# Batch 4's first layer as seven products instead of eight, and a rewritten order of all later work, in an attention and two-layer kernel

## The chip, the cores and the metric

The kernel runs on one core of a Trainium2 chip. Its engines each take their own instructions in order: TensorE (PE in the profile, with its weight loads as PEld), VectorE (DVE), ScalarE (ACT), GpSimd (POOL) and SyncE (SP). They wait for each other through semaphores. SP and POOL issue most of the DMA transfers. The metric is the device time of one execution in microseconds.

## The reference

Inputs are q, k and v of 8 batches, 12 heads, 448 positions and 64 features, and two weight matrices of 768 x 2048 and 2048 x 768, all float32.

```python
scores = scale * np.matmul(q, k.transpose(0, 1, 3, 2))      # scale = 1 / sqrt(64)
attn = np.maximum(scores, 0.0) ** 2 / S                      # no softmax
x = np.matmul(attn, v)             # then heads side by side: 3584 rows of 768
h = x @ w_in
g = 0.5 * h * (1.0 + erf(h * inv_sqrt2))
out = g @ w_out                    # 3584 rows of 768, float32
```

## The kernel before

**Attention.** The loads on POOL's queue turn q, k and v into bfloat16 on their way in. Heads are handled in three groups of four (g = 0 to 2) and keys in seven pieces (i = 0 to 6). One step of `add_steps` is four matmuls into a PSUM tile `ps` (tag "w", three buffers), a relu on ACT or DVE, and a square on DVE. The square goes into one of 14 buffers of `apool`. When the seven steps of a group are there, `add_av` makes 28 matmuls into `pav`, and two copies put the result into `xT`, which is x transposed.

**Turning q and k.** Scores need q and k with features on the partitions. Batches 0 and 1 are turned by TensorE. For batches 2 to 7 `add_T_dma` (line 657) does it with DMA transposes on SP's queue, one for k and one for q of each head group ("turn"), and then a half-swap of q: the upper 64 partitions are copied below and the lower above, either by two DMAs on SP or by two copies on DVE (`swapped`, line 681). A score step needs the turned k and the swapped q of its group. Natural-layout buffers of q and k are single from batch 2 on, so a load of batch b + 1 into them waits for batch b's turns. `add_gate` (line 706) puts a small copy on POOL that waits for a turn, so that loads behind it on POOL wait too.

**First layer, plain.** `add_f1` makes one of 16 tiles of a batch: six matmuls of 448 columns into `psh`, and a GELU on ACT into `h_sb`, a ring that holds two batches.

**First layer, block form.** `add_blocks` and `add_block` split x, w_in and h into 2 x 2 blocks and make them with seven block products instead of eight, at the price of sums. The sums of w_in are made once (`add_wsums`). Those of x are four per batch (`xsum`, tile `xs`). The seven products of one part (six matmuls of 224 columns each, line 999, PSUM tiles `pb` with tag "w") share three bank pairs a, b and c. Between products DVE or ACT takes a bank's content away (`passed`, tile `part`), and ACT makes four GELUs. A batch has four such parts: m4 = 0 and 4, and y = 0 and 1 for the two banks of a tile. A part that needs a buffer of `h_sb` waits until the readers of the batch two before it are done.

**Second layer.** Rows 0 to 255 are made plainly (`add_plain`, line 1268). Then `add_group` makes 256 rows at a time (groups 1 to 13), again with seven products, of eight matmuls of 384 columns (line 1173). Their sums of h are `s_sb`, those of w_out `t_sb`. The results go through `osb` (three buffers) to the output by stores on SP.

**Which batch is made how.** Batches 0 to 4 are plain in the first layer. Batches 5, 6 and 7 are in block form at the end. While attention runs, PE alternates between attention steps and pieces of the two layers. After the last attention there are only block products and groups.

**What sets the order.** Each piece of work is an `Op` with the engines that may do it. The program lists them, and the text `ORDER` says which stands next: a letter for the engine (P, A, D, G for POOL, S for SP) and the number of the `Op` in the order in which the program made them. Every engine works through its own words in that order. The batch-2 turns and swaps have the numbers 228 to 236: for each head group the turn of k, the turn of q, and the swap. So S229 is the turn of q of group 0, D230 its swap on DVE.

Of the kernel before, what the change touches and what calls it, by code (L numbers as in the profile page):

```python
# [9 lines left out]
BF16 = mybir.dt.bfloat16  # L10
# [6 lines left out]
HS = S // 2  # L17
# [69 lines left out]
G0 G1 G3 G4 G1428 G7 G121 A10 P11 D13 G2 A16 P17 D12 P14 G117 D18 P42 P39 G6 P21 D15 P19 A43 G118  # L87
P36 D22 P33 A40 P23 G5 D20 P25 D41 P54 A37 G122 D24 Z1056 D26 A34 P66 P57 D38 A55 D44 G8 P63 P29
P27 A58 D67 P69 P51 D35 A64 P48 D30 P31 D65 A70 P45 D28 D32 A52 P78 D59 G9 P133 D46 A49 P108 D68
D47 P111 A79 P75 D134 P129 A109 D50 P81 P131 D56 A76 P102 D112 P84 G125 A82 D71 P72 D53 A103 G120  # L90
P60 D130 A85 D104 P93 A73 P135 A61 D110 A74 A62 P96 D132 P105 G124 P141 D83 D77 A97 P168 A94 D106
P165 P90 A142 G119 P143 D86 D113 A169 G126 D107 P114 A166 D80 P87 D98 A91 D95 P171 A144 D115 P137
A88 D92 A116 P99 D89 P156 A172 D136 P159 A100 D138 P145 G128 A157 A101 D160 P162 P186 D167 P174
A146 P251 D163 A175 P243 D158 A187 D176 G148 A252 D170 P183 P195 P189 G147 D173 A244 P259 G151
A196 D184 G154 P253 D161 A260 G150 D164 P139 A190 P198 A254 P180 P177 D140 A181 D199 P219 P216
# [4 lines left out]
G153 G238 P350 A357 G149 P348 G270 A292 A351 P285 P300 P303 G272 A349 P354 G241 A301 P364 A304  # L100
A355 P312 P318 P362 A365 P370 D319 D281 A363 D296 P358 A313 D236 D290 A286 P282 P306 A371 P315
P352 A359 D307 P360 A353 P376 A361 P368 A316 A377 D317 P372 D314 A369 D308 P366 D293 A373 P378
A283 A367 D284 P374 S234 A379 D390 P382 D278 S399 A375 D391 D392 P380 D417 D418 D305 G242 G152
D302 D287 G269 S398 P327 P339 D320 P297 G271 D396 G155 A328 D383 P333 G274 P384 D381 G273 D298
A340 A299 D393 A334 D394 P330 P324 P309 D329 P387 D419 A331 D335 A385 S402 A310 D395 D311 S386
A325 P342 P336 S401 P321 D397 D400 D388 A343 D332 P421 A322 D337 A323 P423 D420 D338 D422 S405
P446 P443 D341 P449 P425 D424 D344 A450 S404 S403 S406 P427 G413 D444 G275 A426 G409 S389 D447
P429 D326 D428 P452 P455 P345 A456 D453 P440 P437 D445 P431 D430 A441 D560 P433 D346 A347 D432
S435 P473 A438 P461 P470 D434 S436 P509 G407 G408 G410 A471 D474 P513 D448 G412 A462 S542 D457
A510 G411 P479 D454 P476 P464 G415 A514 P519 D472 D442 G414 A465 D439 P517 A520 D477 P515 A480  # L110
D451 A518 S541 P485 P467 P458 A468 P491 A516 S545 P511 D459 A486 D561 P523 A492 D487 A512 D460
P503 P494 P500 D563 A524 P525 D463 S544 A495 D466 P521 D469 A526 D481 P531 D504 A522 D478 P527
A532 D501 P537 D475 S548 A528 D505 P529 D502 A538 D493 S547 S543 S546 S549 P488 P497 P482 A498
D489 P606 G556 P600 G552 G416 P535 A483 A530 G550 P533 D601 G551 A607 D484 A536 G553 D490 G555
P539 D496 G554 D499 P609 G559 P603 P506 G558 A604 D610 G557 P624 A534 P639 D562 P564 A540 D605
A507 P566 A640 D625 D565 D508 P615 P612 P618 D567 P568 A616 D613 P570 D617 A569 D611 D614 P572
S705 D619 P657 D571 P627 P636 S704 P574 D580 D573 A637 D620 P576 D608 A658 D575 S578 A628 P584
D581 S708 D638 D577 P586 D583 S579 D582 P630 D602 P633 P621 D626 A634 D631 P651 A585 S707 P642
P588 D632 D587 A643 D659 P590 D629 A652 A622 D641 D591 P648 A623 D644 P666 P663 A589 S711 D653
P592 D635 A664 S710 S706 S709 S712 G719 P594 G715 A649 D667 D593 P654 P660 P645 A655 D661 P769  # L120
P763 D595 P596 S598 D725 A770 G713 G714 A646 P672 D764 G716 D597 S599 P674 G718 D665 D650 A673
G717 G721 A647 D656 P772 P778 P775 G720 D662 A675 P678 S868 A776 D779 P676 D668 A773 D771 P766
D777 P787 P669 S867 A767 D788 A679 P781 P790 A677 D774 P682 A670 D723 D768 P684 A782 A671 D724
A683 D765 P680 D783 A791 D780 P796 P799 P784 A681 S871 A800 D797 P793 P802 P688 D803 D804 S870
D798 D789 D792 S874 S873 S869 S872 S875 G882 G722 A785 A685 P686 A794 A689 A786 P811 P823 P805
A687 P690 D795 A806 P692 A691 D824 P698 D726 A812 D807 A693 P696 D801 A699 P814 P817 P808 A697
A815 D818 P820 P906 G878 P694 A809 G876 G877 P702 D907 G879 A695 A810 G881 P700 G880 A821 G884
A703 P826 P829 D822 P912 A701 P727 A827 P729 D828 A728 D813 P731 A913 D730 A830 D816 P733 D819
D825 P921 D831 P909 P832 A910 D922 P918 P936 D732 G885 P735 D734 A833 G883 D911 A919 D834 P924
P915 A937 P737 D736 A916 D925 P930 P933 D938 P942 P739 D743 A931 D738 S741 D744 P747 A934 D745  # L130
D740 S742 P749 D917 A748 D935 S979 P751 D914 A943 D920 D750 S978 P753 D944 A752 D746 S982 P755
D923 D926 D754 P757 D932 D908 P939 P948 P927 D758 S981 A940 D949 P960 P945 D941 P835 A928 D756
D950 A946 P759 A929 S761 D961 S985 D947 P957 P954 P951 A836 D760 S984 S980 S983 S986 A958 D955
P963 P966 P839 D956 A952 S762 D953 A967 P837 D959 A840 P969 D964 P972 P987 A838 D888 P841 A973
P843 D988 D965 A842 D989 P845 A970 D962 A844 D974 P847 D971 A846 D1067 P1002 D968 P990 P975 A1003
D991 A848 P993 P996 P851 D976 A994 A977 P999 D997 P1014 P1005 A852 D1004 P849 D995 D992 P853 D886
A850 D1068 P857 D998 A1000 A854 P855 D1015 A1006 D1001 P1017 D1007 P1026 P1008 D1070 A1027 D1018
P1029 A856 P1011 P859 A858 D1059 A1009 D1028 P863 D1019 A1030 A860 D1031 P865 A1012 D1060 A864
A1010 P1035 D887 P1047 P1020 D1016 A866 P861 A1048 P890 D1021 A1036 A862 D1063 D1022 P1023 P1041
P1044 A891 D1013 P892 A1024 D1042 P1053 A1045 D1025 P1050 P1032 D1069 A1051 D1054 P1038 P1071  # L140
A1033 D1062 P894 D1049 A1072 D1043 P1088 D893 A1039 P1073 A1034 D1066 A895 P1079 A1089 D1040
P1090 D889 P1096 P1075 D1091 P896 D1055 D1074 D1181 P1094 D1052 P1077 D897 P1092 P898 D1095 D1078
P1082 D1064 P1099 P900 D1061 D899 D1097 P902 D1083 D1100 P1105 D1080 D901 S904 P1102 A1076 D1179
P1085 A1106 D1139 P1122 A1093 D1046 A1084 P1107 D1037 P1124 A1123 D903 S905 P1109 A1081 D1086
P1126 D1103 A1087 P1113 D1108 P1130 D1125 A1110 P1128 A1127 D1065 P1111 A1104 D1140 A1098 P1056
D1180 D1129 D1112 P1133 D1131 P1143 D1057 D1114 P1119 D1058 P1136 D1134 D1291 P1116 D1144 P1183
D1120 P1200 D1137 P1185 D1117 P1202 A1184 D1141 A1201 P1191 D1182 P1187 D1203 P1145 D1186 P1189
P1206 P1208 P1147 D1190 D1207 D1146 P1194 D1192 P1211 D1209 P1149 D1195 P1214 D1212 D1148 P1217
D1150 P1197 D1142 P1151 A1218 A1115 D1198 A1118 P1221 D1215 A1135 P1234 D1152 A1121 P1219 A1132
P1236 A1101 A1138 P1153 A1235 D1237 P1238 D1161 P1155 D1220 D1154 S1157 P1240 D1159 P1223 D1156  # L150
S1158 P1163 D1160 D1241 P1245 P1165 D1164 D1224 P1228 P1167 D1166 D1162 D1246 P1169 D1229 D1168
P1225 P1171 D1170 D1253 P1173 D1172 D1226 P1175 D1251 P1242 P1231 A1239 P1204 A1222 P1303 A1227
D1243 P1248 D1176 S1178 A1188 P1320 A1205 D1252 P1295 A1210 D1174 S1177 A1244 D1232 P1312 A1199
D1292 P1255 A1230 D1249 A1296 D1254 A1313 P1297 D1293 A1193 P1314 A1196 P1299 A1256 P1257 A1233
D1298 A1213 D1315 A1216 P1301 P1316 D1258 P1318 P1261 D1319 P1259 D1302 D1304 D1294 P1309 D1262
P1323 A1260 A1250 P1263 D1310 A1247 D1324 P1306 D1321 P1265 D1264 D1307 P1326 P1329 P1346 D1327
P1331 D1271 P1267 A1347 D1272 A1330 P1350 P1348 D1268 S1270 P1333 P1275 D1349 D1266 S1269 D1273
P1277 D1276 P1279 D1274 D1332 D1278 P1352 P1335 A1280 P1281 P1283 D1282 P1285 D1365 D1353 D1336
# [239 lines left out]
def kernel(  # L398
# [738 lines left out]
    def add_group(g):  # L1137
# [116 lines left out]
        for bb in bs:  # L1254
            readers.setdefault(bb, []).extend(mine)
# [287 lines left out]
```

## Time and profile before

| what | us |
|---|---|
| median of 3 runs (lowest, highest) | 369.7 (369.43, 370.05) |
| the profiled execution | 368.93 |
| its span, first to last instruction | 367.2 |
| PE, DVE, ACT, POOL busy | 358.1, 291.2, 191.8, 63.5 |
| psh, plain first layer, 516 matmuls | 96.3 |
| ps and pav, scores and attention output, 756 matmuls each | 47.9 and 36.3 |
| last attention output on PE ends | 263.7 |

A busy time is the union of an engine's instructions. Matmuls overlap, so a single one's duration (0.34 us) is longer than its share of the stream. A DVE instruction of 617 ns is followed by the next after 535 ns. The chain of waits follows the last instruction back to what released it. The timeline gives start, length, engine, line and operands, and in brackets how long the engine had stood idle and what ended that.

### The profile page before, as it was taken

The numbers are of one execution on the slowest core, as the hardware profiler recorded it, in microseconds if no ns is written. First come the engines' busy times: TensorE is split into PE (matmuls) and PEld (weight loads), VectorE is DVE, ScalarE is ACT, GpSimd is POOL, SyncE is SP. The second block draws the span as 40 slices with busy tenths as digits, with TensorE's granted clock in tenths as the row PEclk, the third lists the DMA queues.
The fourth block names the chain that finished last, engine by engine and source line by source line (L and its number), as shares of the span: only waits on it lengthen the run. The fifth ranks groups of instructions, "written<-read, shape, count | busy, mean of one in ns | idle before, by whom it ended". The sixth has DMA issues, their size and how long they took to land.

```text
span 367.2 us, 8476 instructions
## 1 busy us (share of the span) xinstructions
PE 358.1 (98%) x3560; PEld 222.3 (61%) x3560; DVE 291.2 (79%) x488; ACT 191.8 (52%) x312; POOL 63.5 (17%) x101
## 2 busy tenths in 40 slices
PE   8889999999999999999999999999999999999994
PEld 7666654455544555544455544478888787867662
DVE  3999882689996899998579999999977766667753
ACT  4987867637377544678665466951414134133100
POOL 8565134410600700501310000000000000000000
PEclk9999999999999999999999999999999999999998
DMA  9999999999999999999949770000200211022233
GB/s 172 200 200 204 188 141 203 191 197 157 162 258 172 185 167 188 175 247 161 190 68 201 142 158 2 2 2 5 83 2 1 87 48 40 14 73 87 86 86 88
DMA packets 74406, 46.19 MB, mean 126 GB/s; under 512 B 38400, under 2 KB 70912, under 8 KB 74368
## 3 DMA queue, kind: packets, MB, share of 16 engines
q0 software_dynamic: 32912, 22.47, 42.2%
q1 hardware_dynamic: 40816, 22.67, 29.5%
q8 instruction: 28, 0.46, 0.5%
q10 hardware_dynamic: 640, 0.51, 0.4%
q14 instruction: 10, 0.08, 0.1%
HBM read 45.61 MB, written 11.01 MB: 154 GB/s over the span
## 4 chain that ended last, share of the span: by engine, by line
PE 95%; ACT 3%; issue 1%; DVE 0%; DVEq 0%
PE pso L1173 33%; PE psh L855 26%; PE pb L999 13%; PE ps L742 10%; PE pav L803 9%; ACT a_sq L754 3%; PE pso L1268 3%; PE spin L1340 1%; PE tp L638 0%; PE tp L610 0%; DVE qT L516 0%; DVEq L1538 0%; DVE osb L1207 0%; DVE zero L1324 0%
## 5 line engine op out<-in xcount | busy, mean ns | idle before, releaser
L754 ACT ACTIVATE a_sq<-ps 128x896 bf16<-128x896 f32 (+1 forms) x116 | 102.5, 923 | 44.1 <-PE ps L742 41.1
L763 DVE TENSOR_TENSOR a_sq<-a_sq 128x896 bf16<-128x896 bf16 x169 | 97.1, 614 | 8.0 <-ACT a_sq L754 7.7
L855 PE MATMUL psh<-xT,win_sb 128*128 128x448 bf16 (+1 forms) x516 | 96.3, 340 | 0.0
L855 PEld LDWEIGHTS <-win_sb 128*128 128x128 bf16 x516 | 47.9, 98 | 45.9 <-issue 9.8
L756 DVE TENSOR_SCALAR a_sq<-ps 128x896 bf16<-128x896 f32 (+1 forms) x53 | 57.0, 1078 | 16.6 <-PE ps L742 16.4
L1173 PEld LDWEIGHTS <-s_sb 128*128 128x128 bf16 x424 | 40.7, 98 | 25.7 <-issue 1.8
L865 ACT ACTIVATE h_sb<-psh 128x448 bf16<-128x448 f32 x80 | 43.5, 550 | 22.3 <-PE psh L855 22.0
L742 PE MATMUL ps<-qT,kT 64*64 64x448 bf16 (+1 forms) x756 | 47.9, 336 | 1.0 <-ACT a_sq L754 0.4
L1036 DVE TENSOR_TENSOR part<-pb,part 128x448 f32<-128x448 f32 x60 | 35.2, 617 | 13.6 <-PE pb L999 11.5
L1173 PEld LDWEIGHTS <-h_sb 128*128 128x128 bf16 x312 | 29.8, 98 | 20.9 <-issue 3.2
L1173 PE MATMUL pso<-wout_sb,h_sb 128*128 128x384 bf16 x208 | 38.1, 326 | 0.0
L1173 PE MATMUL pso<-wout_sb,s_sb 128*128 128x384 bf16 (+2 forms) x216 | 38.1, 320 | 0.0
L1173 PE MATMUL pso<-t_sb,s_sb 128*128 128x384 bf16 x208 | 38.1, 326 | 0.0
L803 PE MATMUL pav<-a_sq,v_sb 64*64 64x448 bf16 (+1 forms) x756 | 36.3, 329 | 1.3 <-issue 1.1
L1207 DVE TENSOR_TENSOR osb<-pso,p_sb 128x384 f32<-128x384 f32 x39 | 21.5, 551 | 13.0 <-PE pso L1173 11.2
L742 PEld LDWEIGHTS <-kT 64*64 64x64 bf16 x756 | 18.6, 105 | 21.1 <-issue 16.2
L999 PEld LDWEIGHTS <-win_sb 128*128 128x128 bf16 x288 | 27.5, 98 | 2.9 <-issue 0.7
L803 PEld LDWEIGHTS <-v_sb 64*64 64x64 bf16 x756 | 21.1, 107 | 13.0 <-issue 2.3
L1045 ACT ACTIVATE h_sb<-part 128x448 bf16<-128x448 f32 x36 | 18.4, 576 | 19.0 <-DVE part L1036 18.9
L710 POOL COPY gate<-qT 128x16 bf16<-128x16 bf16 x15 | 5.2, 345 | 100.2 <-DMA qT<-nq 79.9
L518 ACT CAST xT<-pav 128x448 bf16<-128x448 f32 (+1 forms) x38 | 18.3, 500 | 7.7 <-PE pav L803 6.3
L999 PEld LDWEIGHTS <-ws 128*128 128x128 bf16 x216 | 20.8, 98 | 1.2
(58 smaller groups left out, 300.5 us busy)
## 6 DMA issues: line engine op xcount, KB each, us to landing
nk<-in_k_dram POOLq DMA_DIRECT2D x23, 224.0 KB, 10.3
nq<-in_q_dram POOLq DMA_DIRECT2D x21, 224.0 KB, 10.2
v_sb<-in_v_dram POOLq DMA_DIRECT2D x5, 672.0 KB, 9.1
qT<-qT SPq DMA_DIRECT2D x28, 112.0 KB, 2.6
out_dram<-osb SPq DMA_DIRECT2D x8, 336.0 KB, 3.0
v_sb<-in_v_dram POOLq DMA_DIRECT2D x9, 224.0 KB, 9.4
out_dram<-osb SPq DMA_DIRECT2D x7, 288.0 KB, 3.1
out_dram<-osb SPq DMA_DIRECT2D x8, 240.0 KB, 3.0
```

The costliest lines, as they stand in the source:

```text
L742: nc.tensor.matmul(ps[64 * j : 64 * j + 64, e, x * w : x * w + w], kT[r, g, i * 128 + 64 * j : i * 128 + 64 * j + 64], moving, start=True, ...
L754: A.activation(ar, ps, AF.Relu, scale=c_att)
L756: V.tensor_scalar(ar, ps, c_att, 0.0, op0=mybir.AluOpType.mult, op1=mybir.AluOpType.max,)
L763: V.tensor_mul(box["a2"][:, :, :used], ar, ar)
L803: nc.tensor.matmul(pav[0][o2 : o2 + 64, e, :w], vt[b][r, 2 * g + e, bass.ts(i, D)], box["a2"][r, y, o : o + w], start=(i == 0), stop=(i == ...
L855: nc.tensor.matmul(ph[:, x * n : x * n + n], win_sb[:, kd, bass.ts(m + x, 128)], xT[b][:, kd, c], start=(kd == 0), stop=(kd == KD - 1),)
L865: A.activation(h_ring()[:, m : m + nm, o + c.start : o + c.stop], box[0][:, :S].rearrange("p (x n) -> p x n", x=nm), AF.Gelu,)
L999: nc.tensor.matmul(bank[name][:, y, z * HS : z * HS + HS], w[:, k, bass.ts(mm, 128)], right()[:, k], start=first and k == 0 and z == 0, st ...
L1036: V.tensor_add(get(to), ps(name), get(other))
L1045: A.activation(h_ring()[:, m : m + 2, o + half[c].start : o + half[c].stop], src().rearrange("p (x n) -> p x n", x=2), AF.Gelu,)
L1173: nc.tensor.matmul(box[bank][:, n0:n1], left()[:, kf], right()[:, kf, n0:n1], start=bool(need) and kf == 0, stop=kf == K2 - 1, skip_group_ ...
L1207: V.tensor_add(out()[:, n0:n1], box[bank][:, n0:n1], other()[:, n0:n1])
```

## The change

Batch 4 moves from the plain form to the block form and into the end: its 16 tiles are no longer spread over attention. The list at the end of the program is built without weaving groups between block products. The x sums of batches 6 and 7 share one buffer, and those of 4 and 5 take the place of kT. Readers and writers of the h ring are now tracked by half batches of 224 rows. `ORDER` is new throughout. In it some half-swaps move from SP to DVE: of the 18, 14 were on SP before and 6 are now. The gates on POOL stand in other places.

```diff
-P245 A178 G123 G127 A220 D217 P207 A179 P210 P204 D191 A246 P261 S229 A211 D208 P247 D182 A205
-S228 D209 A262 D197 P213 P222 P192 D200 S232 A248 P263 D221 A223 D206 P249 D224 A264 D188 P255
-D212 A250 P257 D193 A214 A256 D194 P265 D218 A258 D185 P201 D230 D215 A266 G237 S231 G239 P225
-A202 A203 P276 P279 P267 D233 D226 S235 A277 A227 P291 D280 P288 P294 A268 P356 G240 A295 D289
...
+D181 A199 D188 P216 D178 D197 P245 P219 A220 D179 A217 D185 P247 S228 A246 P210 P204 P207 A211
+A208 A248 S235 D205 P261 S232 P222 P213 D200 D221 D191 A262 P192 A214 P263 S231 P255 A264 D182
+D223 D206 A193 D218 P257 A256 D194 P249 D215 A258 D212 D209 P201 S234 S229 D224 D230 G270 P225
...
@@ -873,7 +875,8 @@
-        old = readers.get(b - 2, [])
+        hs = (0, 1) if half is None else (half,)
+        old = [o for x in hs for o in readers.get((b - 2, x), [])]
...
@@ -952,13 +957,19 @@
-                    tag = "qT" if b == B - 1 else "kT"
-                    box["t"] = tpool.tile([128, 4, K1, HS], BF16, tag=tag, name="xs")
+                    if b < B - 2:
+                        box["t"] = tpool.tile([128, 4, K1, HS], BF16, tag="kT", name="xs")
+                    else:
+                        if not xsums:
+                            xsums.append(
+                                tpool.tile([128, 2, 4, K1, HS], BF16, tag="qT", name="xs2")
+                            )
+                        box["t"] = xsums[0][:, b - B + 2]
...
-        gone = [o for (bb, *_), o in QK.items() if bb == (B - 2 if b == B - 3 else B - 1)]
+        gone = [o for (bb, *_), o in QK.items() if bb == (B - 2 if b == B - 4 else B - 1)]
...
@@ -1433,7 +1450,7 @@
-    F1B = {2: 1, 3: 2, 4: 3, 5: 4}
+    F1B = {2: 1, 3: 2, 4: 3}
...
-    add_wsums(at(B - 1, 1), [F1[B - 4, m, None] for m in range(KF)])
+    add_wsums(at(B - 1, 1), [F1[B - 5, m, None] for m in range(KF)])
...
-    end = woven(add_blocks(B - 3), add_group(7))
-    end += add_group(8)
-    end += woven(add_blocks(B - 2), add_group(9))
-    g10 = add_group(10)
-    end += g10 + woven(add_blocks(B - 1), add_group(11))
-    end += add_group(12) + add_group(13)
+    end = add_blocks(B - 4) + add_group(7)
+    end += add_blocks(B - 3) + add_group(8) + add_group(9)
+    end += add_blocks(B - 2) + add_group(10)
+    end += add_blocks(B - 1) + add_group(11) + add_group(12) + add_group(13)
```

In the old words batch 2's turns stand as S229, S228, S232, S231, S235, and S234 later. In the new ones they stand as S228, S235, S232, S231, S234 and S229, with D230 right behind.

More of the change, by code (lines that the diff above doesn't have):

```diff
@@ L104 @@
[L104 to L145, printed above, removed]
@@ new lines @@
+P297 A328 P333 D392 P339 A334 P382 D298 A375 D329 A340 D317 A299 P330 P324 P309 A325 P380 D417
+D320 A331 D310 A383 D311 D418 D335 P342 D341 P336 P321 D332 S402 D393 P384 A322 D400 S401 A381
+A337 D326 D396 G407 D394 P387 G237 A385 A343 G409 G240 D420 S386 G275 A323 D344 S405 G408 D419
+P443 D338 D388 P446 S404 A444 P421 D395 A447 G412 S389 P449 D397 P345 G411 A450 G242 D445 D403
+A422 P452 P437 A346 S542 P423 D347 A453 A438 P455 D424 P440 P425 D456 A441 D442 P473 P470 A426
+P461 D454 P427 D462 A474 A471 P429 D439 D457 D428 P464 P479 D430 P476 A480 D448 P431 D451 A465
@@ new lines @@
+D1020 P1041 A1040 D1030 D1008 P1058 A1057 D1011 P868 D1059 P1024 D1042 P1045 A1025 A1026 P1060
+D1129 D1031 D1032 D867 P1062 P1043 P1047 D1063 A1044 D1029 P870 A1061 D1046 P1064 D1034 P1050
+P1067 D1048 D1065 P1073 D1051 P1090 D1068 P1053 D1033 P1075 A1074 A1091 A1049 P1092 D1054 P1094
+D1093 P1077 D1076 A1078 A1066 P1070 D871 P1079 D1071 P1096 D869 A1072 A1095 A1055 P1081 D1097
+A1052 S872 S873 P1098 D1080 A1069 P1131 D1082 P1084 D1128 A1083 P1101 D1099 P1148 A1100 P1104
+D1085 D1102 A1149 P1087 A1103 D1331 A1132 P1133 D1105 D1088 A1086 P1150 P1135 D1134 A1106 P1139
@@ L166 @@
+P1417 D1416 A1379 D1423 P1419 D1418 D1424 P1383 D1420 P1400 S1422 P1427 S1421 P1429 D1428 D1384
+D1425 P1431 D1430 A1385 A1368 P1433 D1432 A1362 D1401 D1426 P1435 A1402 D1434 D1445 P1437 D1436
+D1443 P1439 D1438 D1444 S1441 P1447 D1440 S1442 P1449 D1448 P1451 D1450 D1446 P1453 D1452 S1463
+P1455 D1454 P1457 D1456 P1459 D1458 P1460 D1461 D1462 S1465 S1464 S1466
 """
@@ L939, in add_wsums @@
             WS[m0] = {1: s1, 2: s2, 3: s3, 4: s4}
+    xsums = []
     def add_blocks(b):
@@ L973, in add_blocks @@
         TS = {1: t1, 2: t2, 3: t3, 4: t4}
-        old = readers.get(b - 2, [])
         atoms = []
@@ L979, in add_blocks @@
                 ms = range(m4 + 2 * y, m4 + 2 * y + 2)
-                todo.append(add_block(b, m4, y, ms, bank, x, t, TS, xs, old, half))
+                todo.append(add_block(b, m4, y, ms, bank, x, t, TS, xs, half))
             for p in zip(*todo):
@@ L986, in add_blocks, with add_block @@
         return atoms
-    def add_block(b, m4, y, ms, bank, x, t, TS, xs, old, half):
+    def add_block(b, m4, y, ms, bank, x, t, TS, xs, half):
         tmp = {}
@@ L1051, in gelu @@
             d = 0.19 + 0.00069 * S
+            old = readers.get((b - 2, c), [])
             o = sch.add((("ACT", d, d + 0.14),), fn, deps + old, frees=frees, bias=GELU_BIAS)
@@ L1144, in h @@
             return h_ring()[:, i * K2 : i * K2 + K2, o : o + 128]
-        done = [o for (bb, *_), o in GL.items() if bb in bs]
+        hs = {t // HS for r in rows for t in (r[0], r[-1])}
+        done = [
+            o for (bb, m, h), o in GL.items()
+            if bb in bs and (isinstance(m, int) and h is None
+                             or 2 * bb + (h if isinstance(m, int) else m[1]) in hs)
+        ]
         sums = SUMS[0] + SUMS[1]
@@ L1253, in add_group @@
                 sch.add((("SP", 0.6, 2.8),), store(0, c, [nc.scalar, nc.sync]), [o])
-        for bb in bs:
-            readers.setdefault(bb, []).extend(mine)
+        for t in sorted({t // HS for r in rows for t in (r[0], r[-1])}):
+            readers.setdefault(divmod(t, 2), []).extend(mine)
         return [(1.3, o) for o in (p1, p6, p2, p7, p5, p4)] + [(1.3 / len(p3), o) for o in p3]
@@ L1289, in add_plain @@
         plain.append(op)
-        readers.setdefault(bb, []).append(op)
+        for t in sorted({128 * t // HS, (128 * t + 127) // HS}):
+            readers.setdefault(divmod(t, 2), []).append(op)
         return op
```

102 lines of the change are left out of this document (62 added, 40 removed).

## The prediction

> **What bounds the kernel now.** I read the page first, then the chain of waits, then the queues where batch 2 begins.
>
> ```profile
> span 367.2 us, 8476 instructions
> PE 358.1 (98%) x3560; PEld 222.3 (61%) x3560; DVE 291.2 (79%) x488; ACT 191.8 (52%) x312; POOL 63.5 (17%) x101
> PE 95%; ACT 3%; issue 1%; DVE 0%; DVEq 0%
> ```
>
> TensorE is busy for 98% of the span and makes 95% of the chain that ends last. From about 20 us to its last product at 362 us it is fed without a break, so work that leaves PE shortens the time, and any new wait of PE lengthens it one for one. The prices are in the chain of waits (start, us, engine and line, count):
>
> ```profile
> 0.99 4.98 PE spin L1340 x45
> ...
> 45.64 5.78 PE psh L855 x30
> 51.42 2.77 PE pav L803 x56
> 54.19 0.38 PE ps L742 x8
> ...
> 104.46 0.69 PE ps L742 x12
> 105.15 2.38 PE psh L855 x12
> ...
> 214.41 0.95 PE ps L742 x12
> ...
> 298.11 4.60 PE pb L999 x48
> ```
>
> A plain first-layer tile (six matmuls on line 855) takes 1.135 us: two take 2.38 and five 5.78, each with 0.11 ahead. A block product (six matmuls of 224 columns, line 999) takes 4.60 / 8 = 0.575. A score step (four matmuls, line 742) takes 0.19, and three take 0.69: going from attention to the other layers, or back, costs 0.11 to 0.12. The 0.95 at 214.41 is the one wait of the body: 0.26 more than three steps.
>
> Batch 2 is the first whose q and k are turned by the DMA queue of SP. This is what SP, POOL and DVE do before PE reaches it (timeline):
>
> ```profile
> 37.30 1.42 POOL L569 DMA_DIRECT2D v_sb<-in_v_dram  x2 [1.53 <-DMA win_sb<-in_moe_w_in_dram]
> 39.88 1.33 SPq L665 DMA_TRANSPOSE qT<-nq  x1
> 41.27 2.86 SPq L665 DMA_TRANSPOSE kT<-nk  x1
> 44.17 4.05 SPq L665 DMA_TRANSPOSE qT<-nq  x1
> 48.27 1.30 SPq L665 DMA_TRANSPOSE kT<-nk  x1
> 49.61 1.30 SPq L665 DMA_TRANSPOSE qT<-nq  x1
> 50.91 0.79 DVE L516 COPY qT<-qT 64x896 bf16<-64x896 bf16 x2
> 51.76 0.65 POOL L710 COPY gate<-qT 128x16 bf16<-128x16 bf16 x1 [13.03 <-DVE qT L516]
> 54.02 0.55 PE L742 MATMUL ps<-qT,kT 64*64 64x448 bf16 x8
> ```
>
> The reader is to see the order: q of head group 0 is turned first (issued 39.88), DVE swaps its halves at 50.91, and PE takes its first scores of batch 2 at 54.02, three microseconds after the swap could begin. The loads set the pace: the two v loads issued at 37.30 and 38.03 landed 9.4 and 10.1 us later, the last at 48.2, and the first turn, issued at 39.88, landed only after 8.8 us, at 48.7. The fifth, issued at 49.61 with nothing before it, landed after 3.0, at 52.6.
>
> **The change, part by part.** *Batch 4 in block form.* 16 tiles of 1.135 leave PE, 18.16 us. In come 4 blocks of 7 products, 28 x 0.575 = 16.10. PE: -2.06.
>
> *Order on PE.* Counted in the built programs, the sequence changes between attention and the other layers 95 times before and 103 times after. 8 x 0.115 = +0.92.
>
> *Other engines.* The built program gives DVE 20 more passes over block banks (617 ns each), 4 more x sums (498), 16 more half-swaps of qT (405, until now DMAs), and 9 fewer relus (1086). DVE rows overlap by 0.08 (four products of 617 ns take 2.22 us in the timeline). With that, batches 3 to 6 hold 98 us of DVE work against 108 of PE (before: 99 against 120); a block's seven products take PE 4.0 us and DVE 2.7. I put these at nothing: PE's own work hides them. If that cover were gone, only what exceeds PE would count. Bounds: below, no gain, since PE does not wait for these today; above, the swaps' 16 x 0.405 = 6.5 us if each stood on the path; nearest is the row of line 516 copies, whose four in batch 2 hide today. Inside the blocks the closest pair is batch 5's c bank, 1.15 us from one product's end to the next that needs its pass (0.62); the tail's pairs, 1.30 apart with passes of 0.55, run without a wait. I take 0.
>
> *Batch 7's swaps.* The 0.26 at 214.41 ended when the SP swap for its head group 0, issued at 212, landed; the new order issues that swap before two of the six turns. I take -0.26 (bounds -0.26 and 0).
>
> *Turns of batch 2.* In the new ORDER the six turns stand as k of group 0, q of 2, q of 1, k of 1, k of 2, and last q of group 0. The copy that swaps group 0 waits for the sixth turn, and PE's first score step for that copy. The fifth turn needs the load of k of group 2. Before, that load stood behind two gates on POOL (issued at 53.99); now it follows the v loads directly, at about 38.8. Loads around it landed 1.2 to 1.4 us apart, so I expect it at 48.2 + 1.3 = 49.5. Then the fifth turn is issued at 49.5 and the sixth 1.3 later (rows of 48.27 and 49.61), at 50.8 to 51.5, and it lands 3.0 to 3.2 us after that: 53.9 at the least, 54.4 likely. If the fifth turn's issue is slow, as the 2.86 and 4.05 us rows are while loads are outstanding, 55.4. The swap adds 0.9 (0.79 and a hand-over): PE gets its scores at 54.8 to 56.3, 55.3 likely.
>
> When does PE ask? Ahead of batch 2 the new order has one plain tile less (-1.13) and two more changes (+0.23): 54.02 - 0.90 = 53.1. So PE waits 1.7 to 3.2 us; I take 2.2, the side of the rows with an empty queue. All engines behind are in order: DVE's relus of batch 2 stand behind the swap but wait for PE anyway; the gate to the output weights, batch 3's q load, stands on POOL until the sixth turn has landed (54.4 for 51.76), so the weights come some 3 us later; they landed at 70 and 78, and their first readers on PE stand at 79 and 87. That cover holds with 5 us or more.
>
> *Tail.* The last products change places: the 256-column piece first, then the 128-column one, and on SP two larger stores now follow that piece's store. SP issues of 0.32 to 0.42 us each move the last from 1.0 to about 1.2 us after PE's end, while the last add is 0.12 shorter. I take +0.1 (bounds -0.1 and +0.6, the stores being issued at 361.33 before).
>
> Sum: -2.06 + 0.92 - 0.26 + 2.2 + 0.1 = +0.9 us. The profiled execution took 368.93 (span 367.2), 0.8 below the median of the runs, 369.7. So 369.8 in that execution, 370.6 by the median.
>
> **The rivals.**
>
> *A. The sixth turn comes in time (faster).* DMA traffic before 48 us is shared, and turns could slip between loads. If the sixth lands by 52.2, PE never waits. For it: a later turn of batch 2, issued at 60.69, landed at 71.0, ahead of loads issued before it. Against: it cannot be issued before the load of k of group 2 has landed. Then -1.3: 368.4.
>
> *B. The transfers don't keep up later.* PE reaches batch 5 some 10 us and batch 7 some 14 us earlier in its own work, while the 16 DMA engines' share (packet times summed, so above one) is 1.13 to 1.25 up to 180 us and 0.84 from there to 215. Against: batch 7's loads had landed by 200 and its turns waited for stores on SP, 16 SP transfers are gone, and the loads are issued earlier. A second wait like batch 2's, 2.2, gives 372.8.
>
> *C. The array slows after the wait.* The 45 spin matmuls of 128 columns took 0.111 each, the 48 of 224 columns at 298 us 0.096: per column the start runs at half the rate. If the wait put the array back there for 3.4 us, work of 1.7 would be lost: 372.3. The one idle stretch of before, 1.3 us at 18.6 to 20, was followed by no slow row (PEclk 1.00). [...]
>
> **How the numbers follow.** Forecast 0.57, A 0.18, B 0.17, C 0.08. Within the forecast the wait's bounds give 369.9 to 372.1. Measurement tells about 0.2%, 0.74 us, from no change. Of the forecast's 0.57 some 0.2 has a wait near 1.7 and stays within that; A is faster but for 0.02. So faster 0.16, same 0.22, slower 0.62. The range takes in A and B: 368.3 to 373.2.
>
> **What would show it.** After: on line 742 an idle stretch of PE of 1.7 to 3.2 us just before the first scores of batch 2, ended by DVE's qT copy; on SP the sixth turn issued after 50; the gates gone from that place on POOL. The groups of pb should count 672 matmuls for 504, those of psh 420 for 516, and PE should again be without waits from 60 us on. The prediction falls if that wait is under 1 us (then A), or if PE stands still at a later batch's first scores or between block products.

## The result, and the profile after

The changed kernel takes 370.44 us by the median of 21 runs (369.97 to 373.96); the kernel before, in 21 runs beside them, 369.4 (368.65 to 370.61). The ratio of their means is 1.0043, with a 95% interval of 1.0027 to 1.0060: slower, by 1.0 us between the medians and 1.6 between the means, because the changed kernel has some runs far above its median. The forecast was 370.6, 0.9 above the time before.

The profiled execution took 370.31 us, with a span of 368.6 (before: 368.93 and 367.2). First the page: PE is busy for 357.1 us, 1.0 less than before, in a span that is 1.4 longer.

```profile
span 368.6 us, 8647 instructions
PE 357.1 (97%) x3632; PEld 227.7 (62%) x3632; DVE 298.3 (81%) x511; ACT 205.0 (56%) x333; POOL 64.1 (17%) x101
PE 90%; DMA 3%; SPq 2%; POOL 1%; DVE 1%; issue 1%; ACT 1%; DVEq 0%; POOLq 0%
```

PE's share of the chain that ended last fell from 95% to 90%. SP's queue (2%) and the landing of a turn of q (1%) have come in; the larger part of the DMA's 3% is a v load at 6 to 14 us, where the chain before went through ACT. The chain of waits says where the turns stand in it (start, us, what):

```profile
43.44 0.53 PE ps L744 x8
...
43.99 1.10 DVE a_sq L758
...
45.44 3.44 SPq L667
...
48.93 1.32 SPq L667
...
50.30 1.30 SPq L667
...
51.69 3.16 DMA qT<-nq
...
54.87 0.39 DVE qT L518
...
55.29 0.40 DVE qT L518
...
55.73 0.57 PE ps L744 x6
56.30 2.38 PE psh L857 x12
```

From 45.1 to 55.7 the end of the kernel hangs on SP's turns of batch 2 and the swap, and not on PE. The third turn's issue lasts 3.44 us, until 48.88 (the load of k of group 2 lands at 48.85); then the fourth to sixth follow each other without a pause, at 48.93, 50.30 and 51.69. The sixth, q of group 0, lands at 54.85, DVE swaps, PE gets its scores. The timeline shows the hole on PE:

```profile
51.21 2.84 PE L805 MATMUL pav<-a_sq,v_sb 64*64 64x448 bf16 x56
51.69 10.29 SPq L667 DMA_TRANSPOSE qT<-nq  x2
...
54.87 1.86 DVE L518 COPY qT<-qT 64x896 bf16<-64x896 bf16 x4 [2.81 <-DMA qT<-nq]
55.31 0.98 PE L744 MATMUL ps<-qT,kT 64*64 64x448 bf16 x8 [1.26 <-DVE qT L518]
55.42 0.72 POOL L464 DMA_DIRECT2D nq<-in_q_dram  x1 [15.50 <-DMA qT<-nq]
```

PE is idle for 1.26 us. Counted from start to start of matmuls, the first scores come 1.42 late, and the second step another 0.23, since it needs the other half of the swap: 1.65 in all. On POOL the load of batch 3's q has waited 15.5 us for the sixth turn; the gates that stood there before are gone, as announced. From 56 us to its last product no wait of PE is listed.

### The profile page after: what moved, and what is told of

It reads as the page before. It is cut to its first block, busy times and chain, and to the rows that moved or that the text cites. A ratio compares the mean times of both kernels' runs of the same rounds, so it can differ in the third digit from the quotient of the medians.

```text
span 368.6 us, 8647 instructions
## 1 busy us (share of the span) xinstructions
PE 357.1 (97%) x3632; PEld 227.7 (62%) x3632; DVE 298.3 (81%) x511; ACT 205.0 (56%) x333; POOL 64.1 (17%) x101
## 4 chain that ended last, share of the span: by engine, by line
PE 90%; DMA 3%; SPq 2%; POOL 1%; DVE 1%; issue 1%; ACT 1%; DVEq 0%; POOLq 0%
PE pso L1189 33%; PE psh L857 19%; PE pb L1009 17%; PE ps L744 9%; PE pav L805 8%; PE pso L1284 3%; DMA v_sb<-in_v_dram 2%; SPq L667 2%; DMA qT<-nq 1%; POOL nk L553 1%; POOL nq L464 1%; ACT a_sq L756 0%; PE tp L640 0%; DVE a_sq L758 0%; PE tp L612 0%
## 5 line engine op out<-in xcount | busy, mean ns | idle before, releaser
L756 ACT ACTIVATE a_sq<-ps 128x896 bf16<-128x896 f32 (+1 forms) x125 | 109.8, 918 | 33.5 <-PE ps L744 33.3
L857 PE MATMUL psh<-xT,win_sb 128*128 128x448 bf16 (+1 forms) x420 | 77.6, 337 | 0.6 <-issue 0.5
L1046 DVE TENSOR_TENSOR part<-pb,part 128x448 f32<-128x448 f32 x80 | 46.8, 619 | 15.9 <-PE pb L1009 14.6
L758 DVE TENSOR_SCALAR a_sq<-ps 128x896 bf16<-128x896 f32 (+1 forms) x44 | 47.0, 1077 | 11.9 <-PE ps L744 11.4
L744 PE MATMUL ps<-qT,kT 64*64 64x448 bf16 (+1 forms) x756 | 48.7, 336 | 2.7 <-DVE qT L518 1.3
L867 ACT ACTIVATE h_sb<-psh 128x448 bf16<-128x448 f32 x64 | 34.7, 550 | 18.5 <-PE psh L857 18.4
L1055 ACT ACTIVATE h_sb<-part 128x448 bf16<-128x448 f32 x48 | 25.7, 575 | 17.6 <-DVE part L1046 17.4
L1009 PEld LDWEIGHTS <-ws 128*128 128x128 bf16 x288 | 27.7, 98 | 1.0
L464 POOL DMA_DIRECT2D nq<-in_q_dram x24 | 17.8, 740 | 51.5 <-DMA qT<-nq 38.4
```

The source lines that it names most:

```text
L744: nc.tensor.matmul(ps[64 * j : 64 * j + 64, e, x * w : x * w + w], kT[r, g, i * 128 + 64 * j : i * 128 + 64 * j + 64], moving, start=True, ...
L756: A.activation(ar, ps, AF.Relu, scale=c_att)
L758: V.tensor_scalar(ar, ps, c_att, 0.0, op0=mybir.AluOpType.mult, op1=mybir.AluOpType.max,)
L857: nc.tensor.matmul(ph[:, x * n : x * n + n], win_sb[:, kd, bass.ts(m + x, 128)], xT[b][:, kd, c], start=(kd == 0), stop=(kd == KD - 1),)
L867: A.activation(h_ring()[:, m : m + nm, o + c.start : o + c.stop], box[0][:, :S].rearrange("p (x n) -> p x n", x=nm), AF.Gelu,)
L1009: nc.tensor.matmul(bank[name][:, y, z * HS : z * HS + HS], w[:, k, bass.ts(mm, 128)], right()[:, k], start=first and k == 0 and z == 0, st ...
```

## The experiments

Each kernel was timed in turn with the kernel before on the same chip, whose median was 369.33 to 369.49 in all sets. `S`, `D`, `A`, `P`, `G` in the diffs are words of ORDER; "..." stands for the words between.

### The place of one turn

```diff
-S228 ... S235 ... S232 ... S231 ... S234 S229
+S229 S228 ... S235 ... S232 ... S231 ... S234
```

> The changed kernel with one word moved: the turn of q of group 0 of batch 2 is issued first of the six on SP instead of last. Theory (the place of that turn makes the wait): it lands near 50, DVE swaps before PE asks at 53.9, and the wait before batch 2's first scores (1.42 us idle and 0.23 in the second step) goes: span 368.6 - 1.65 = 367.0, the median of the runs 1.5 to 1.7 below the changed kernel's. If the upper runs of the changed kernel (371 to 374 for a median of 370.4) come from longer waits at that place, they go too, and the runs lie within 1 us or so, as those of before. Rival (transfers before batch 2 are late whatever the order, the k turn or the loads): a wait of 1 us or more stays at the first scores, span 368.0 to 368.6.

Measured: median 368.51 (367.89 to 370.28), a ratio to the kernel before of 0.9983 (0.9966 to 0.9999); span 366.7. The timeline of this kernel at the place:

```profile
51.20 2.84 PE L805 MATMUL pav<-a_sq,v_sb 64*64 64x448 bf16 x56
52.08 2.81 DVE L518 COPY qT<-qT 64x896 bf16<-64x896 bf16 x4
53.87 0.55 PE L744 MATMUL ps<-qT,kT 64*64 64x448 bf16 x8
54.35 2.44 PE L857 MATMUL psh<-xT,win_sb 128*128 128x448 bf16 x12
```

The score steps follow the attention output without a gap, and 1.9 us have gone from the median, 2.3 from the mean. So one word of the new order makes the change slow; without it, the rest makes the kernel faster by 0.85. The rival falls: no wait is left there. No run lies above 370.3, so the long upper tail went with the wait, but the runs still spread over 2.4 us and not over the 1 that was expected (those of the kernel before beside them over 2.8). The turn landed at 50.7.

### The same turn fifth

```diff
-... S231 ... S234 S229
+... S231 ... S229 S234
```

> The changed kernel with the turn of q of group 0 fifth instead of last, ahead of the turn of k of group 2. Theory: it takes the issue time of the fifth turn, 50.3 instead of 51.7, lands 3.2 to 3.6 us later at 53.5 to 53.9, and with the swap (0.9) PE gets its scores at 54.4 to 54.8 instead of 55.3: a wait of 0.5 to 0.9 us is left, span 367.7 to 368.1. Here the fifth turn needs no late load, so it may be issued as soon as SP is free; rival (the wait belongs to the load of k of group 2, which lands at 48.85, and not to the place): no wait is left, 367.0.

Measured: 369.51 (368.81 to 370.77), ratio 1.0000 (0.9983 to 1.0017); span 367.2. The turn was issued at 50.24 and landed at 53.53, as the theory has it; scores came at 54.0, and of the wait 0.14 and 0.23 us were left, less than the 0.5 to 0.9 expected because the first half of the swap came 0.45 us after the landing and not 0.9. A place further back in SP's queue makes that turn 1.3 to 1.4 us later. The fifth place was issued at the same time in both kernels, whether its turn needed the late load (50.30) or not (50.24): that load does not hold the fifth turn itself. It had landed at 48.8 in both.

### A longer wait at the same place

```diff
-S229 D224 D230
+S229 D224 S230
```

> The changed kernel with the half-swap of group 0 of batch 2 done by two DMAs on SP instead of two copies on DVE, so that PE waits longer at the same place. The turn lands at 54.85; the two transfers land some 2.3 to 3.2 us after it (the swap of batch 7 in the kernel before: issued at 212, ended the wait at 214.4), so PE gets scores at 57.2 to 58.1 instead of 55.3, an idle stretch of 3.3 to 4.2 us. Theory that the array slows after an idle stretch (the granted clock fell to half 2.4 to 3.2 us after PE's last product in both profiles): the profile shows PEclk under 1.00 behind the wait, plain tiles at up to 2.27 us instead of 1.14 for some 3 us, and the span is 368.6 + 1.9 to 2.8 + up to 1.7 = 370.5 to 373.1. Rival (an idle stretch inside the kernel costs only itself): clock 1.00 behind the wait, tiles at 1.14, span 370.5 to 371.4.

Measured: 376.2 (375.91 to 376.4), ratio 1.0180 (1.0150 to 1.0209); span 374.5, above both expectations. The two transfers landed 2.2 and 4.4 us after the turn, the second later than I had allowed, so PE waited twice (3.09 and 1.60 us). And the clock fell. The profile in stretches of 3.4 us (start and end, length, PE busy, PEld, DVE, ACT, POOL, PEclk, DMA share, GB/s):

```profile
53.56:56.97 3.41, 0.32 (x6) 0.14 (x3) 0.00 (x0) 0.76 (x2) 1.93 (x3) 1.00 0.40 65
56.97:60.38 3.41, 1.81 (x10) 0.47 (x8) 0.00 (x0) 0.86 (x2) 3.41 (x5) 0.50 1.16 173
60.38:63.80 3.42, 3.42 (x10) 1.37 (x9) 0.00 (x0) 1.85 (x4) 1.69 (x4) 0.50 1.19 162
63.80:67.21 3.41, 3.41 (x32) 1.29 (x31) 2.46 (x3) 2.00 (x3) 1.35 (x2) 1.00 1.29 189
```

After 3.1 us of idleness the granted clock is 0.50 for 6.8 us. From the start of two plain tiles to the next score step it took 4.33 us (59.79 to 64.12), elsewhere 2.38. The theory holds; the rival, an idle stretch that costs only itself, falls.

### The relu that stood in the wrong place

The timeline of the changed kernel showed ACT idle with work lying ready (score steps and relus):

```profile
40.25 0.36 PE L744 MATMUL ps<-qT,kT 64*64 64x448 bf16 x4
...
41.80 0.38 PE L744 MATMUL ps<-qT,kT 64*64 64x448 bf16 x4
42.23 1.73 ACT L756 ACTIVATE a_sq<-ps 128x896 bf16<-128x896 f32 x2 [2.35 <-PE ps L744]
43.37 1.02 PE L744 MATMUL ps<-qT,kT 64*64 64x448 bf16 x12
```

The step at 40.25 waits for its relu until the step at 41.80 has had its own, because ACT's words stand that way round. Three steps then took 1.02 us where 0.76 is usual. In q0_first_relu the turn is first, as in q0_first, and:

```diff
-P219 A220 D179 A217
+P219 A217 D179 A220
```

> As the first of these runs (q of group 0 first), and two words on ACT exchanged: the relu of the fifth step of batch 1's third group ahead of that of the sixth, the order in which PE makes the two. Theory: in the changed kernel ACT stood idle for 2.35 us at 39.9 to 42.2, waiting for the later step while the earlier one lay ready, all three score buffers were then full, and PE lost about 0.7 us between 43.4 and 46.1 in score steps of 0.4 instead of 0.19. With the exchange this goes: 0.4 to 0.7 us below the first of these runs. Rival (ACT and DVE together can't take score steps any faster there): the short waits stay, and the two kernels take the same time within 0.15 us.

Measured: 367.99 (367.65 to 369.55), ratio 0.9964 (0.9949 to 0.9979), 0.5 below q0_first. In its timeline each relu follows its step, and three steps take 0.76 again:

```profile
41.07 0.36 PE L744 MATMUL ps<-qT,kT 64*64 64x448 bf16 x4
41.48 0.92 ACT L756 ACTIVATE a_sq<-ps 128x896 bf16<-128x896 f32 x1 [0.79 <-PE ps L744]
42.61 0.38 PE L744 MATMUL ps<-qT,kT 64*64 64x448 bf16 x4
43.05 0.92 ACT L756 ACTIVATE a_sq<-ps 128x896 bf16<-128x896 f32 x1 [0.65 <-PE ps L744]
44.18 0.76 PE L744 MATMUL ps<-qT,kT 64*64 64x448 bf16 x12
```

### The changed kernel again, and the exchange of relus alone

> The changed kernel as it is, beside the next one on the same chip. Theory: most runs at 370.0 to 370.8 with a mean granted clock of 0.995 to 1.00, and some (5 of the 21 shown) at 372 to 374 with a clock of 0.991 to 0.994: in these the wait before batch 2 was longer and the clock fell to half, as in swap_on_sp, where it stood at half for 6.8 us and the mean clock was 0.986. Were the upper runs of another cause, their clock would be as that of the others.

Measured on this chip: 372.08 (370.16 to 375.37, seven runs), ratio 1.0064 (1.0039 to 1.0089). Not most but two of the seven lie at 370.0 to 370.8; four lie above 372. Of these, two have a clock of 0.987 and 0.992. The other two have 0.995, which runs of 370.1 and 370.2 in the other sets have as well, so for them a lower clock is not shown. The profiled execution was the one of 375.37, clock 0.987:

```profile
50.32 2.84 PE L805 MATMUL pav<-a_sq,v_sb 64*64 64x448 bf16 x56
...
56.68 1.86 DVE L518 COPY qT<-qT 64x896 bf16<-64x896 bf16 x4 [5.51 <-DMA qT<-nq]
57.12 1.37 PE L744 MATMUL ps<-qT,kT 64*64 64x448 bf16 x8 [3.96 <-DVE qT L518]
...
58.43 4.66 PE L857 MATMUL psh<-xT,win_sb 128*128 128x448 bf16 x12
```

Same program, same place: PE came 0.9 us earlier than in the first profile, the turn landed 1.8 later (56.66), the wait was 3.96 us and the two tiles behind it took twice their time (4.66 us for 2.44). The loads were late here: the one of k of group 2 landed at 50.89 instead of 48.85, and the third turn's issue lasted until 50.90 instead of 48.88. The clock stood at 0.50 from 56.64 to 63.46.

> The changed kernel with the two words on ACT exchanged (relu of the fifth step of batch 1's third group ahead of that of the sixth), and the turn of q of group 0 left last. With that turn first, the exchange was worth 0.5 us. Theory: here it is worth nothing, because PE asks for batch 2's scores 0.5 to 0.65 us sooner and waits so much longer for the same turn (idle 1.9 to 2.1 us instead of 1.42); the fast runs keep their time, 370.2 to 370.5, and as the idle stretch comes nearer to the 2.4 to 3.2 us after which the clock fell at the end of the kernel, the share of runs above 371.5 with a clock under 0.995 grows past the changed kernel's 6 in 21. Rival (the exchange works for itself): median 0.4 to 0.6 below the changed kernel's.

The edit is the two words on ACT, with the turn left last:

```diff
-P219 A220 D179 A217
+P219 A217 D179 A220
```

Measured: 371.76 (369.83 to 374.73, eleven runs), ratio 1.0066 (1.0042 to 1.0090). The exchange that gained 0.5 us in the kernel with the turn first shows no gain here: beside the 372.08 of seven runs of the changed kernel a difference of 0.3 can't be told from none. Of eleven runs eight are above 371.5, all eight with a clock of 0.995 or less. That is more than in the first set of the changed kernel (six of 21, of which five under 0.995 and one at 1.00), but the set on the same chip has four of seven, so that the share grew by the exchange is not shown. In the profiled execution the turn landed at 54.49, 0.36 earlier than in the first profile; PE had asked at 53.29, 0.8 earlier. The wait was 1.67 us, under the 1.9 to 2.1 expected, and the clock fell 1.5 us after PE had gone on:

```profile
53.04:56.45 3.41, 1.69 (x19) 0.65 (x12) 1.78 (x4) 1.49 (x3) 1.39 (x2) 1.00 0.30 58
56.45:59.86 3.41, 3.41 (x10) 1.20 (x8) 0.00 (x0) 1.94 (x4) 3.41 (x5) 0.50 1.08 128
59.86:63.28 3.42, 3.42 (x32) 1.42 (x32) 2.72 (x3) 2.00 (x3) 2.31 (x4) 1.00 1.05 146
```

### The price of a change between attention and the other layers

In eight places a tile or product was put ahead of the last of three attention steps, such as:

```diff
-P318 ... P312 ... P300 ... P354
+P318 ... P312 ... P354 P300
```

> As q0_first_relu, and in eight places of batches 2 to 5 the first tile or product behind three attention steps is put ahead of the last of them: 119 changes between attention and the other layers instead of 103, with the same work. Theory: each change costs what the trace shows between two matmuls of different kind, 0.093 into attention and 0.10 out of it: 16 x 0.097 = 1.55 us more, 369.5 by the median for 368.0. Rival (the gaps at the changes are paid anyway, by steps that would else wait for score buffers): under 0.5 us.

Measured: 372.25 (371.79 to 373.39), ratio 1.0078 (1.0060 to 1.0097): 4.3 above q0_first_relu, far more than 1.55. The moves did two things. The changes cost what they cost elsewhere: between two matmuls of a plain tile 0.189 us pass from start to start, between its last one and a score step 0.282; into the tile 0.282 instead of 0.18. But the moves also tore score steps from the attention output that needs their squares, and twice a tile of the first layer waits for a GELU on ACT. The list of PE's waits after 56 us, empty for the changed kernel, has entries:

```profile
PE pav L805 <- DVE a_sq L758: 0.6, 1, 0.6
PE psh L857 <- ACT h_sb L867: 0.4, 2, 0.2
PE pav L805 <- ACT a_sq L756: 0.4, 1, 0.4
```

From start to start these and one late score step come to 2.4 us; with 16 x 0.097 = 1.55 that is 4.0 of the 4.3 between the medians. So the rival (under 0.5) falls, and the price per change rests on the intervals in the trace, not on this run's total.

### One change of layer less

```diff
-P216 ... P245 P219
+P216 P219 ... P245
```

> As q_first_relu (q of group 0 first, relus exchanged), and the sixth score step of batch 1's third group directly behind the fifth, without the half tile of layer one between them, as the kernel before has it: 101 changes between attention and the other layers instead of 103. Theory: 2 x 0.1 = 0.2 us less, 367.8 by the median for 368.0. Rival (the score buffers fill up when steps stand closer): nothing gained, or a new short wait at 40 to 46 us.

Measured: 368.41 (367.71 to 369.31), ratio 0.9969 (0.9956 to 0.9983), where q0_first_relu had 0.9964: no gain that can be seen. The expectation missed. Of its rival, "nothing gained" holds, but not the place of the short wait. No wait is left at 40 to 46 us; the timeline of this kernel has one later:

```profile
58.15 2.75 SPq L667 DMA_TRANSPOSE qT<-nq  x1
59.19 0.57 PE L744 MATMUL ps<-qT,kT 64*64 64x448 bf16 x8 [1.21 <-DMA kT<-nk]
```

Here PE waits for the turn of k of group 1. It stands fifth when q of group 0 is simply pulled to the front, is issued at 51.28, and lands at 59.15, while batch 3's q and the output weights, issued from 50.92 on, are under way. In q0_first_relu, too, it was issued behind that load of q, and landed after 6.8 us (here 7.9); in q0_first and sixteen_changes it was issued ahead of it, and landed after 4.9 and 5.2.

### The turns in the old order

Here all six turns stand as in the kernel before; the two relus on ACT are exchanged as well.

```diff
-S228 ... S235 ... S232 ... S231 ... S234 S229
+S229 S228 ... S232 S231 S235 ... S234
-P219 A220 D179 A217
+P219 A217 D179 A220
```

> The changed kernel with all six turns of batch 2 on SP in the order of the kernel before (q0, k0, q1, k1, q2, k2), and the two relus on ACT exchanged. Theory: with q of group 0 first alone, the turn of k of group 1 stood fifth and landed at 55.5 to 59.2, behind the load of batch 3's q and the first output weights, which start earlier there; in one_pair_less PE waited 1.21 us for it at 59.2. Fourth, it lands near 53, well ahead of its first reader at 55 to 59, and the time is that of q0_first_relu where that did not wait, 367.7 to 368.0, with no run above 369. Rival (the k turn was an accident of one profile): the same spread as q0_first_relu, 367.65 to 369.55.

Measured: 367.83 (366.93 to 368.33), ratio 0.9952 (0.9933 to 0.9971). The turn of k of group 1 landed at 52.87, no run of eight is above 368.4, and the list of PE's waits from 38 us to the end is empty. Its page:

```profile
span 365.2 us, 8647 instructions
PE 355.7 (97%) x3632; PEld 227.0 (62%) x3632; DVE 298.5 (82%) x511; ACT 205.2 (56%) x333; POOL 64.2 (18%) x101
```

This is 0.5% under the kernel before, with PE busy for 1.4 us less than in the changed kernel as it was. By the median it can't be told from q0_first_relu (367.99), and the next kernel, with the same order of turns, has one run of 369.5: that the place of the k turn narrows the spread is not shown.

Next, on top of this, the pair of steps of one_pair_less, and on POOL batch 4's v load moved behind a gate:

```diff
-G416 G410 G554 G413
+G410 G554 G413 G416
```

(POOL's words alone.)

> As old_turns; besides, the fifth and sixth score steps of batch 1's third group stand together as in one_pair_less, and on POOL batch 4's v load comes behind the gate on batch 3's third group instead of ahead of the gate on its second, so that the last turn of batch 4 (k of group 2), which landed 12 to 17.5 us after its issue at 128 to 139 and kept PE waiting 0.6 to 1.1 us in three profiles, is not behind it. Theory: 0.2 us for two changes less and 0.2 to 0.6 in the executions that waited there: 367.3 to 367.7 by the median, without a wait at 132. Rival (that turn is late for the two k loads and the stores, not for v): the same landing and time as old_turns but for the 0.2.

Measured: 367.7 (367.44 to 369.5), ratio 0.9953 (0.9939 to 0.9967). The median can't be told from that of old_turns. The last turn of batch 4 (k of group 2) landed at 126.7, 11.3 us after its issue, but it landed at 127.2 in old_turns too: whether the v load had delayed it in the three executions that waited is not shown.

### The wait filled with work

```diff
-A250 P279
+A250 Z5632 P279
```

(Z5632 stands for 5632 columns of zeros, 11 times 512.)

> The changed kernel with 11 matmuls of 512 columns on zeros put on PE ahead of batch 2's first scores, into the wait; their result is not used. Estimated from the second layer's 384 columns in 0.163 us they take 11 x 0.217 = 2.4 us, so PE is busy from 53.9 to 56.3, and where the swapped q came at 55.3 it starts 1.0 us later than it could. Theory (the upper runs are those in which the clock fell to half after the wait): PE is hardly idle there, the clock stays at 1.00, and the runs lie close together at 371.2 to 371.8, with none above 373 and none with a mean clock under 0.995; the upper half of the changed kernel's runs gets faster through more work. Rival (the upper runs are late transfers alone, the clock follows): the same spread as the changed kernel, moved up by up to 1 us.

> The changed kernel beside filled_wait on the same chip: a third to two thirds of its runs above 371.5 with a clock of 0.995 or less, as in the two earlier sets (6 of 21 and 4 of 7), the others at 370.0 to 371.

Measured: filled_wait 372.33 (370.55 to 373.09, six runs), ratio 1.0069 (1.0046 to 1.0091); the changed kernel beside it 370.62 (369.89 to 372.23, twelve runs), ratio 1.0031 (1.0018 to 1.0045). With the matmuls on zeros no run has a clock under 0.996, and in the profile PE is busy through the place, as the theory has it; but with one low run in twelve beside it, six runs do not show that the filling prevented others. The rest of the theory failed: the runs are not close together, four of six lie at 372 to 373 with a clock of 0.996 to 0.999, and two are at 370.6. The rival's forecast fits: the lowest and highest run are 0.7 and 0.9 above those of the changed kernel beside it. So something other than the clock spreads the runs by 2 us or so. The time at which the turn comes is the candidate: with that turn last it landed at 54.5 to 54.9 in five profiles and at 56.7 in one. None of the slow runs of filled_wait was profiled, so this stays unproven. Filling the wait is no cure. The changed kernel itself had one run of twelve under 0.995 here (372.23, 0.991), and two above 371.5, fewer than expected.

## Why the prediction came out right, step by step

*The wait.* This was the step that decided, and the mechanism is shown: put the turn first and 1.9 us leave the median, put it fifth and about half of that goes. Each link came close: the load of k of group 2 landed at 48.85 (49.5 forecast), the sixth turn was issued at 51.69 (50.8 to 51.5) and landed at 54.85 (53.9 to 55.4), PE had its scores at 55.31 (55.3). That this last time was hit to the hundredth is luck: the turn landed 0.45 later than the likely 54.4, and the first scores needed only the first half of the swap, 0.46 instead of 0.9. One link was wrong in kind: I had the fifth turn wait for that load. What lasted until the load had landed was the issue of the third turn, and the fifth followed the fourth at once. In the kernel before it was the same: the third turn's issue ended at 48.22, the last v load landed at 48.18. In q0_first and old_turns it ended 0.3 and 0.4 us ahead of the last landing, so that the landing itself ends it is not shown. The wait itself was 1.65 us in the profiled execution, just under the 1.7 to 3.2 that I gave, because PE asked at 53.9 and not at 53.1. Of these 0.8 us, 0.3 were there at 38.0 already, when PE turned batch 1's last q (38.01, before 37.69); 0.5 were lost to the relus below. Over all runs the turn's place was worth 1.9 us by the median and 2.3 in the mean; I had taken 2.2, but the mean holds the runs with a lower clock, which I had priced apart, so that agreement says little.

*Other engines at nothing.* This is the term that failed. "I put these at nothing: PE's own work hides them" held for the sums of batches 3 to 6, from which I argued, and PE has no wait there in the profile. It did not hold at 43 to 46 us in batch 1, where I had not looked at the order of ACT's words: two relus in the wrong order were worth 0.5 us once the wait behind them was gone. With the wait in place they cost nothing more, since PE then only waits less for the turn. So this error and the size of the wait partly hid each other, and that the total came out within 0.2 us is in part luck.

*PE's work.* From batch 2's first scores to PE's last product the kernel before takes 308.01 us, and the changed one with the old turns 307.49 (q0_first 307.51): -0.5. The terms of the forecast for that stretch are 15 plain tiles, 28 products, six changes and the wait at 214: -0.5 too. In the trace a plain matmul is followed by the next after 0.1898 us and a product's after 0.0959, so 96 and 168 of them give -18.22 + 16.11 = -2.11 (-2.06 forecast). The groups are those announced (operands, count, busy, mean ns):

```profile
L1009 PE MATMUL pb<-xT,win_sb 128*128 128x224 bf16 x192 | 22.5, 259 | 0.0
L1009 PE MATMUL pb<-xs,win_sb 128*128 128x224 bf16 x192 | 22.0, 259 | 0.0
L1009 PE MATMUL pb<-xs,ws 128*128 128x224 bf16 x192 | 21.8, 259 | 0.0
L1009 PE MATMUL pb<-xT,ws 128*128 128x224 bf16 x96 | 11.3, 259 | 0.0
```

That is 672, and the idle time before them is 0.0 throughout: the passes, x sums and swaps that DVE got are hidden.

*The changes of layer.* 0.097 each on the intervals, for 0.115: eight cost 0.78, not 0.92.

*Batch 7's swaps and the tail.* The 0.26 at 214 is gone. From PE's last product to the end of the span there are 5.31 us for 5.13: +0.2, for +0.1.

*Sum.* Without the wait I had -1.3 us against the kernel before. q0_first_relu, which has neither the wait nor the relus in the wrong order, is 1.37 below it by the medians. With both, the kernel changed by +1.04 (median) where +0.9 was forecast.

*The rivals.* A (the turn comes in time) was wrong in the four profiles that have that turn last and its swap on DVE with nothing put into the wait: PE was idle for 1.26 to 3.96 us. B happened on a small scale: a turn of batch 4 kept PE waiting for 0.4 to 0.9 us in three profiles (375.37, relu_only, q0_first_relu), and not in the first. There 0.58 to 1.12 us pass from start to start of two score matmuls, where 0.19 is usual; the 0.6 to 1.1 in the expectation of old_turns_plus are these whole intervals. C I had taken as one way or the other, with 0.08, beside one idle stretch of the kernel before that no slow row followed (18.99 to 20.07 in its chain of waits: 1.08 us, not 1.3). The 3.4 us at half rate in its 372.3 stood in no row of before; relu_only then had 3.41 us at 0.50 behind the wait, swap_on_sp and the execution of 375.37 6.8. Whether it comes is a matter of the execution: in 8 of the 40 runs of the changed kernel the mean clock was under 0.995, and these are all at 371.9 or above; of the other 32, two (both at 0.995) are above 371.8. Of the 8, only the one of 375.37 has a profile that shows the clock fall behind the wait. The 90 runs of the kernel before beside the experiments have none under 0.995 and none above 371.2. The low runs are why the ratio of means, 1.0043, is larger than the forecast (0.9 of 368.9, 1.0024): without the five of them among the first 21 it would be 1.0028.

## What to carry to other kernels

Where several transfers wait on one queue, their order should be that of their readers: a place further back was 1.3 to 1.4 us here, and one word made a gain of 0.2% (q0_first) into a loss of 0.4%. A shorter path to a wait that a transfer ends showed no gain here (relu_only), so find that wait before pricing what lies ahead of it; and when it is gone, look for the next late transfer, in one profile here the k turn. Sums of an engine's work over a stage do not show whether it stands ready in the right order: read the words of the engine that answers next, too.

## What the runs showed of the hardware that was not expected

In these profiles the edges of the granted clock lie whole multiples of 3.41 us apart. In relu_only the clock rose at 59.86 and fell, after PE's last product, at 370.48: 310.6 us, or 91 times 3.413. In the execution of 375.37 the two edges are 307.2 apart, 90 times. In the first profile of the changed kernel the spin matmuls follow each other after 0.107 us until 4.60 and after 0.056 from 4.68 on, and the clock fell at 366.45; 106 times 3.413 ahead of that is 4.64, between the two. The stretches below are counted from these edges in steps of 3.413, also where the clock does not change. One in relu_only in which PE was busy for 1.69 of 3.41 us was followed by one at half rate; the longest idle time in it was 1.67 us, and PE had been at work again for 1.5. Stretches with 2.11 (the first profile of the changed kernel), 2.21 (one_pair_less) and 2.25 (changed_beside) were followed by full rate, as here:

```profile
52.43:55.84 3.41, 2.11 (x42) 1.08 (x36) 0.91 (x3) 1.86 (x4) 0.42 (x1) 1.00 0.50 86
55.84:59.25 3.41, 3.41 (x30) 1.38 (x26) 0.90 (x3) 3.11 (x5) 3.41 (x5) 1.00 0.74 91
```

Busy time alone does not decide it. At the end of sixteen_changes a stretch with 1.52 was followed by full rate, too: the clock stood at 1.00 through the next one, in which PE had nothing to do:

```profile
363.15:366.56 3.41, 1.52 (x18) 1.22 (x15) 1.18 (x3) 0.00 (x0) 0.00 (x0) 1.00 0.14 39
366.56:369.97 3.41, 0.00 (x0) 0.00 (x0) 0.00 (x0) 0.00 (x0) 0.00 (x0) 1.00 0.46 134
```

Those 1.52 us are matmuls of 128 x 128; of the 1.69 in relu_only some 1.2 are of 64 x 64. That their size is what counts is not tested here. On the way back, in the execution of 375.37 a stretch at half rate with 2.93 busy, nearly half of it 64 x 64, was followed by a second one, so that the half rate lasted 6.8 us; in relu_only one with 3.41 busy was followed by full rate.

So a wait of about 1.5 us cost itself alone in one execution and more in another. Behind the wait of 1.67 us in relu_only, with 3.41 us at half rate, the two plain tiles took 4.13 us for 2.44, 1.7 more; behind one of 1.5 in changed_beside's profile the clock stayed at 1.00. The first lay within one stretch (53.04 to 56.45), the second across the start of one (53.83); whether that decides is not shown. Which share of the spread of the runs is the clock's and which the transfers' own stays open: filled_wait, with no run under 0.996, still spreads over 2.5 us.
